# Attention followed by an MLP-mixer on one core: giving every engine a fixed order and preparing q and k pair by pair, several pairs ahead

## The chip, the cores and the metric

The kernel runs on one core of a Trainium2 chip. The metric is the device time of one execution in microseconds (us). Every number below comes from such a run, or from the trace of one profiled execution. The trace's own length, from the first to the last recorded instruction, is called the span; in every execution on record it is 1.7 to 2.5 us shorter than that execution's device time.

The engines are named as in the profile: PE does matrix multiplications (PEld is its loading of weights), DVE is the vector engine, ACT the one for activation functions, POOL is GpSimd, and SP issues most of the loads. Each engine works through its own list of instructions in order. An instruction that waits for another engine holds up everything behind it on its own list: in a timeline below, a sum that waits 6.64 us on DVE holds up a copy that was long ready. Two memories are named: PE writes its results into PSUM, and other engines copy them out; the other tiles lie in SBUF.

## The reference

```python
# B=8 batches, H=12 heads, S=448 positions, E=64; D = H*E = 768
q_n = q / (norm(q, axis=-1) + 1e-06)
k_n = k / (norm(k, axis=-1) + 1e-06)
attn = softmax(q_n @ k_n.T / tau)             # tau = 0.1
x = (attn @ v).transpose(0, 2, 1, 3).reshape(B, S, D)

h = relu(x.T @ w_tok1) @ w_tok2               # 448 -> 256 -> 448, over the positions
u = x + h.T
out = u + relu(u @ w_ch1) @ w_ch2             # 768 -> 1536 -> 768, over the channels
```

## The kernel before

The twelve heads of a batch are six pairs, so there are 48 pairs in all; three pairs make a half batch ("half"), of which there are 16. A round is one pass of the loop, for one pair. For each pair, PE transposes the normalised q and k (`tpose`), computes scores in two groups (`score`), ACT takes their exponential, and PE multiplies by v (`pv`). The mixer's work for a batch is queued when its attention is done and is fed to PE in small portions between the parts of later pairs. Before any of it, q and k must be normalised. This is called preparation here: squares, their sums, a square root by way of Ln and Exp, a reciprocal, and the scaling.

```python
def prep(n, lo, hi, sq_eng):                     # a whole half at a time
    ...
    for i, src in enumerate((qf, kf)):
        ...
            nc.gpsimd.tensor_mul(out=sq[:, i], in0=src, in1=src)
    nc.vector.tensor_reduce(out=ssq[:], in_=sq[:]..., axis=AXX.X, op=ALU.add)
    nc.scalar.activation(out=nr[:], in_=ssq[:], func=AF.Ln, bias=tiny[:])
    nc.scalar.activation(out=nr[:], in_=nr[:], func=AF.Exp, scale=0.5)
    nc.vector.tensor_scalar_add(out=rnf, in0=nr[:], scalar1=EPS_NORM)
    nc.vector.reciprocal(out=rnf, in_=rnf)
    for j in range(lo, hi, 2):                   # three pairs
        ...                                      # qn, kn <- q, k times rn, on GpSimd

def score(i, cg):                                # twice for each pair; psS has one buffer
    ...
    nc.scalar.activation(out=st["pt"][:, cg], in_=psS[:, :, :, 0:S], func=AF.Exp, scale=inv_tau)

with tc.manual_schedule(engines={PE, mybir.EngineType.Pool}):
    ...
    for i in range(NP_ALL + 1):
        ...
        if i % HP == 2 and i // HP + 2 < NHALF:
            prep(i // HP + 2, 0, 6, "pool")
            cast_v(i // HP + 2)                  # on DVE
        ...
            score(i, 0)
            left = feed(left + quota * 0.25)     # mixer work of an earlier batch
            if i:
                pv(i - 1, 0)
            ...
```

PE and GpSimd follow the order of the program text; the order on DVE and ACT is chosen by a scheduler when the kernel is built.

Of the kernel before, what the change touches and what calls it, by code (L numbers as in the profile page):

```python
# [7 lines left out]
FP32 = mybir.dt.float32  # L8
FP16 = mybir.dt.float16
AF = mybir.ActivationFunctionType  # L10
ALU = mybir.AluOpType
AXX = mybir.AxisListType
PE = mybir.EngineType.PE

ACT_SET_LN_EXP = 6

# [1 line left out]
def _bcast_free(ap: bass.AP, n: int) -> bass.AP:  # L18
    new_ap = list(ap.ap) + [[0, n]]
    return bass.AP(tensor=ap.tensor, offset=ap.offset, ap=new_ap)  # L20
# [3 lines left out]
def kernel(  # L24
# [12 lines left out]
    nc = tc.nc  # L37

    B, H, S, E = q.shape
# [3 lines left out]
    SC = 112  # L43
    NCH = S // SC
# [6 lines left out]
    HP = 3  # L51
# [5 lines left out]
    COLS = (0, 128, 256, S - 128)  # L57

    cst = ctx.enter_context(tc.tile_pool(name="cst", bufs=1))
    stage = ctx.enter_context(tc.tile_pool(name="stage", bufs=1))  # L60
    qkv = ctx.enter_context(tc.tile_pool(name="qkv", bufs=2))
    nrm = ctx.enter_context(tc.tile_pool(name="nrm", bufs=2))
    att = ctx.enter_context(tc.tile_pool(name="att", bufs=3))
    ptp = ctx.enter_context(tc.tile_pool(name="ptp", bufs=3))
    xp = ctx.enter_context(tc.tile_pool(name="xp", bufs=2))
    mix = ctx.enter_context(tc.tile_pool(name="mix", bufs=2))
    outp = ctx.enter_context(tc.tile_pool(name="outp", bufs=3))
# [19 lines left out]
    NV = 3  # L87
# [28 lines left out]
            nc.gpsimd.dma_start(out=wc2t[:, 6 * i:6 * i + 6, :],  # L116
                                in_=moe_w_ch2[768 * i:768 * (i + 1)].rearrange("(t p) d -> p t d", p=128))

    def load_half(n, split=False):
        b, h0 = n // 2, 6 * (n % 2)  # L120
        qt = qkv.tile([SC, 6, NCH, E], FP32, name=f"qh_{n}", tag="qh")
        kt = qkv.tile([SC, 6, NCH * E], FP32, name=f"kh_{n}", tag="kh")
        vs = qkv.tile([SC, 6, NCH * E], FP32, name=f"vs_{n}", tag="vs")
        for lo, hi in (((0, 2), (2, 6)) if split else ((0, 6),)):
            nc.sync.dma_start(out=qt[:, lo:hi].rearrange("p g c e -> p (g c) e"),
                              in_=q[b, h0 + lo:h0 + hi].rearrange("g (c p) e -> p (g c) e", p=SC))
            nc.sync.dma_start(out=kt[:, lo:hi],
                              in_=k[b, h0 + lo:h0 + hi].rearrange("g (p c) e -> p g (c e)", c=NCH))
        nc.sync.dma_start(out=vs[:], in_=v[b, h0:h0 + 6].rearrange("g (p c) e -> p g (c e)", c=NCH))
        half[n] = dict(q=qt, k=kt, vs=vs, vt=vts[n % NV])  # L130

    def prep(n, lo, hi, sq_eng):

        hf = half[n]
        g = hi - lo
        qf = hf["q"][:, lo:hi].rearrange("p g c e -> p (g c) e")
        kf = hf["k"][:, lo:hi].rearrange("p g (c e) -> p (g c) e", e=E)
        sq = nrm.tile([SC, 2, g * NCH, E], FP32, name=f"sq_{n}_{lo}", tag="sq", bufs=1)
        for i, src in enumerate((qf, kf)):
            if sq_eng == "act":  # L140
                nc.scalar.activation(out=sq[:, i], in_=src, func=AF.Square)
            else:
                nc.gpsimd.tensor_mul(out=sq[:, i], in0=src, in1=src)  # L143
        ssq = nrm.tile([SC, 2 * g * NCH], FP32, name=f"ssq_{n}_{lo}", tag="ssq")
        nc.vector.tensor_reduce(out=ssq[:], in_=sq[:].rearrange("p a g e -> p (a g) e"),  # L145
                                axis=AXX.X, op=ALU.add)
        nr = nrm.tile([SC, 2 * g * NCH], FP32, name=f"nr_{n}_{lo}", tag="nr")
        nc.scalar.activation(out=nr[:], in_=ssq[:], func=AF.Ln, bias=tiny[:])
        nc.scalar.activation(out=nr[:], in_=nr[:], func=AF.Exp, scale=0.5)
        rn = nrm.tile([SC, 2, g, NCH], FP32, name=f"rn_{n}_{lo}", tag="rn")  # L150
        rnf = rn[:].rearrange("p a g c -> p (a g c)")
        nc.vector.tensor_scalar_add(out=rnf, in0=nr[:], scalar1=EPS_NORM)
        nc.vector.reciprocal(out=rnf, in_=rnf)
        for j in range(lo, hi, 2):
            qn = att.tile([SC, NCH, 2, E], FP16, name=f"qn_{n}_{j}", tag="qn")
            kn = att.tile([SC, NCH, 2, E], FP16, name=f"kn_{n}_{j}", tag="kn")
            for i, (dst, src) in enumerate(((qn, hf["q"][:, j:j + 2]),
                                            (kn, hf["k"][:, j:j + 2].rearrange("p g (c e) -> p g c e", e=E)))):
                nc.gpsimd.tensor_tensor(out=dst[:].rearrange("p c g e -> p g c e"), in0=src,  # L159
                                        in1=_bcast_free(rn[:, i, j - lo:j - lo + 2], E), op=ALU.mult)  # L160
            pipe[3 * n + j // 2] = dict(qn=qn, kn=kn)

    def cast_v(n):
        hf = half[n]
        nc.vector.tensor_copy(out=hf["vt"][:, :, :, 0:E].rearrange("p g c e -> p (g c) e"),  # L165
                              in_=hf["vs"][:].rearrange("p g (c e) -> p (g c) e", e=E))

    def tpose(i):
        st = pipe[i]
# [134 lines left out]

    NP_ALL = B * NPAIR
    queue = []

    def feed(budget):

        while queue and budget > queue[0][0] / 2:  # L310
            t, fn = queue.pop(0)
            fn()
            budget -= t
        return budget

    with tc.manual_schedule(engines={PE, mybir.EngineType.Pool}):
        load_half(0, split=True)
        prep(0, 0, 2, "act")
        load_half(1)
        prep(0, 2, 6, "act")  # L320
        cast_v(0)
        weights_tok()
        prep(1, 0, 6, "pool")
        cast_v(1)
        weights_ch1()
        tpose(0)
        for i in range(NP_ALL + 1):
            b, pj = i // NPAIR, i % NPAIR
            left = 0.0
            if i % HP == 1 and i // HP + 2 < NHALF:  # L330
                load_half(i // HP + 2)
            if i % HP == 2 and i // HP + 2 < NHALF:
                prep(i // HP + 2, 0, 6, "pool")
                cast_v(i // HP + 2)
            if i == 2:
                weights_ch2()
            quota = sum(t for t, _ in queue) / (NPAIR - pj + 1) if queue else 0.0
            if i == NP_ALL:
                pv(i - 1, 0)
                pv(i - 1, 1)  # L340
            else:
                score(i, 0)
                left = feed(left + quota * 0.25)
                if i:
                    pv(i - 1, 0)
                left = feed(left + quota * 0.25)
                if i + 1 < NP_ALL:
                    tpose(i + 1)
                score(i, 1)
                left = feed(left + quota * 0.25)  # L350
                if i:
                    pv(i - 1, 1)
                left = feed(left + quota * 0.25)
            if pj == 0 and i:
                first, second = mixer_units(b - 1)
                queue += braid(first, out_units(b - 2) if b >= 2 else []) + second
        queue += out_units(B - 1)
        feed(1e9)
# [35 lines left out]
```

## Time and profile before

| | before |
|---|---|
| device time, median of 3 runs (lowest to highest) | 551.6 us (551.0 to 552.3) |
| span of the profiled execution | 547.6 us |
| PE busy | 445.7 us, 81% |
| first matmul of the mixer (psR) | 66.2 us after the start |
| from there to the end of the span | 481.5 us |
| time at half clock, as far as recorded | 85.6 us |

These are lines of the page of the kernel before: part 1 (busy time and share of the span for each engine), part 2 (40 equal slices; a digit is the busy share in tenths, and PEclk is the granted clock), and part 4 (the chain of work that ended last, by engine).

```profile
...
PE 445.7 (81%) x4136; PEld 267.8 (49%) x4136; DVE 225.7 (41%) x415; ACT 235.7 (43%) x259; POOL 186.7 (34%) x145
...
PE   1546884977997889697977969889795999999996
...
PEclk9999586989898979899896989989897999999999
...
PE 59%; POOL 16%; DVE 14%; issue 5%; ACT 4%; DMA 1%; POOLq 0%; ACTq 0%
...
```

PE is busy for 81%, and nothing else comes near. But only 59% of the chain is PE: another 30% is GpSimd and DVE, which means that the end of the kernel waited for their work and not for PE's. The clock row dips again and again.

The windows of the kernel before (length, then the busy us of each engine with its instruction count, then granted clock, DMA share and GB/s):

```profile
...
80.00:120.00 40.00, 27.43 (x283) 15.89 (x281) 18.54 (x33) 20.61 (x23) 22.96 (x16) 0.83 0.42 96
...
400.00:440.00 40.00, 32.58 (x313) 19.00 (x311) 14.71 (x29) 18.89 (x21) 13.59 (x10) 0.87 0.06 21
440.00:480.00 40.00, 40.00 (x411) 25.15 (x408) 15.42 (x36) 18.00 (x18) 2.05 (x2) 1.00 0.12 41
...
```

After 440 us, when no preparation is left, PE is busy all the time at full clock.

The timeline around the last preparation of the kernel before shows why (start, us, engine, line, operation, tiles written and read; in brackets, how long the engine had been idle and who released it):

```profile
...
411.41 2.75 POOL L143 TENSOR_TENSOR sq_0_4734<-qh_4596 112x1536 f32<-112x1536 f32 x1
...
414.11 2.75 POOL L143 TENSOR_TENSOR sq_0_4734<-kh_4597 112x1536 f32<-112x1536 f32 x1
416.89 3.35 DVE L145 TENSOR_REDUCE ssq_0_4737<-sq_0_4734 112x48 f32<-112x3072 f32 x1 [6.64 <-POOL sq_0_4734 L143]
...
420.25 0.59 DVE L243 CAST ut_2_3774<-psU_5_4718 128x448 f16<-128x448 f32 x1
...
420.90 0.53 PE L249 MATMUL psG_0_4726<-ut_2_3774,wc1t 128*128 128x448 f16 x1 [6.67 <-DVE ut_2_3774 L243]
...
```

GpSimd squares q and k of a whole half, 2.75 us each. DVE stands idle in front of the sum for 6.64 us, because the sum is next on its list, and then needs 3.35 us for it. Behind the sum stands the copy `ut_2`, which empties a PSUM tile of the mixer and which PE needs. PE therefore waits for 6.67 us. Afterwards it runs at half clock: the six matmuls of the psG group that follows at 422 us take 2.36 us of the chain, and 1.14 us where the clock is full. The Trainium skill, "TensorE: Matmul & The Clock Gate", Part 1, has it that an idle window of about 3.4 us drops the PE to half its clock, and that about 3.4 us of work restore it. The size agrees: in this trace the half clock comes in stretches of 3.4, 6.8, 10.2 and 13.7 us.

The longest waits of PE from 66 to 440 us in the kernel before (tile, line, releaser; total us, times, longest us):

```profile
...
PE psG_0_911 L249 <- DVE ut_0_766 L243: 8.2, 1, 8.2
PE psG_0_3243 L249 <- DVE ut_1_2291 L243: 6.7, 1, 6.7
PE psG_0_4726 L249 <- DVE ut_2_3774 L243: 6.7, 1, 6.7
...
```

All waits of PE in this stretch add up to 63 us, and most of the long ones are of this kind: 48 of the 63 us fall into times in which DVE waits for the squares of a whole half or is summing them.

### The profile page before, as it was taken

Reading aid. Unit: us, or ns where it says so; the run is one execution under the profiler, and the core shown is the slowest. Engines: PE = TensorE matmul, PEld = TensorE weight load, DVE = VectorE, ACT = ScalarE, POOL = GpSimd, SP = SyncE. Lnnn points to the kernel's source line nnn. Section 1 sums busy time; section 2 is a strip of 40 time slices with the busy share of each in tenths; the row PEclk is TensorE's granted clock in tenths of the full one; section 3 lists DMA queues with packets and bytes.
Section 4 is the critical chain, followed back from the end, with each engine's and each line's share of the span. In section 5 each row is a group of like instructions: output and inputs, shape, how many; then the busy total and the mean of one; then the engine's idle time right before and its main releaser. Section 6 shows DMA issues by size and latency. Waiting matters only on the chain.

```text
span 547.6 us, 9482 instructions
## 1 busy us (share of the span) xinstructions
PE 445.7 (81%) x4136; PEld 267.8 (49%) x4136; DVE 225.7 (41%) x415; ACT 235.7 (43%) x259; POOL 186.7 (34%) x145
## 2 busy tenths in 40 slices
PE   1546884977997889697977969889795999999996
PEld 0324552544653546354543536545462556656553
DVE  3468484355434344434434344433553233313100
ACT  4435442663346534274434733356343653451221
POOL 2854946525252513325251351515324210000000
PEclk9999586989898979899896989989897999999999
DMA  9969994614170604506070241802200001100102
GB/s 194 225 148 225 230 231 101 152 48 107 56 182 0 152 30 122 118 10 142 30 196 15 56 97 60 209 1 54 77 30 29 1 2 59 57 2 29 59 30 87
DMA packets 72841, 50.02 MB, mean 91 GB/s; under 512 B 44448, under 2 KB 68448, under 8 KB 72800
## 3 DMA queue, kind: packets, MB, share of 16 engines
q1 hardware_dynamic: 69408, 44.05, 32.9%
q0 software_dynamic: 3392, 5.37, 5.5%
q8 instruction: 32, 0.52, 0.4%
q14 instruction: 9, 0.07, 0.0%
HBM read 43.78 MB, written 11.01 MB: 100 GB/s over the span
## 4 chain that ended last, share of the span: by engine, by line
PE 59%; POOL 16%; DVE 14%; issue 5%; ACT 4%; DMA 1%; POOLq 0%; ACTq 0%
DVE vt_102 L165 2%; POOL sq_0_4330 L143 1%; POOL sq_0_3996 L143 1%; POOL sq_0_2847 L143 1%; POOL sq_0_3569 L143 1%; POOL sq_0_3251 L143 1%; POOL sq_0_2513 L143 1%; POOL sq_0_1086 L143 1%; POOL sq_0_776 L143 1%; POOL sq_0_2104 L143 1%; POOL sq_0_1382 L143 1%; POOL sq_0_4734 L143 1%; POOL sq_0_1776 L143 1%; PE psF_0_1_2161 L268 1%; DVE vt_100 L165 1%
## 5 line engine op out<-in xcount | busy, mean ns | idle before, releaser
L249 PEld LDWEIGHTS <-wc1t 128*128 128x128 f16 x576 | 53.9, 102 | 71.8 <-issue 31.0
L268 PEld LDWEIGHTS <-gt_0_767 128*128 128x128 f16 x168 | 16.1, 101 | 16.7 <-issue 7.7
L268 PEld LDWEIGHTS <-gt_1_2292 128*128 128x128 f16 x168 | 15.9, 101 | 14.3 <-issue 4.9
L268 PEld LDWEIGHTS <-gt_2_3775 128*128 128x128 f16 x168 | 15.6, 99 | 13.4 <-issue 3.9
L268 PEld LDWEIGHTS <-gt_3_5228 128*128 128x128 f16 x168 | 15.9, 98 | 9.6
L217 PEld LDWEIGHTS <-w1t 128*128 128x128 f16 x128 | 11.6, 102 | 13.7 <-issue 8.5
L249 PE MATMUL psG_0_911<-ut_0_766,wc1t 128*128 128x448 f16 x6 | 1.6, 384 | 8.2 <-DVE ut_0_766 L243 8.2
L173 PE MATMUL pst_188<-id_89,qn_0_127 112*128 112x112 f16 x4 | 0.6, 294 | 9.4 <-POOL qn_0_127 L159 9.4
L268 PE MATMUL psF_0_1_2161<-wc2t,gt_0_767 128*128 128x384 f16 x12 | 4.0, 520 | 4.6 <-DVE ost_0_2086 L274 4.6
L249 PE MATMUL psG_0_3243<-ut_1_2291,wc1t 128*128 128x448 f16 x6 | 1.6, 383 | 6.7 <-DVE ut_1_2291 L243 6.7
L249 PE MATMUL psG_0_4726<-ut_2_3774,wc1t 128*128 128x448 f16 x6 | 1.6, 382 | 6.7 <-DVE ut_2_3774 L243 6.7
L274 DVE COPY ost_0_5917<-psF_0_0_5918 128x384 f32<-128x384 f32 x1 | 0.6, 558 | 15.2 <-PE psF_0_0_5918 L271 15.2
L145 DVE TENSOR_REDUCE ssq_0_3572<-sq_0_3569 112x48 f32<-112x3072 f32 x1 | 3.4, 3352 | 7.1 <-POOL sq_0_3569 L143 7.1
L145 DVE TENSOR_REDUCE ssq_0_3254<-sq_0_3251 112x48 f32<-112x3072 f32 x1 | 3.4, 3353 | 6.6 <-POOL sq_0_3251 L143 6.6
L145 DVE TENSOR_REDUCE ssq_0_4737<-sq_0_4734 112x48 f32<-112x3072 f32 x1 | 3.4, 3352 | 6.6 <-POOL sq_0_4734 L143 6.6
L203 PEld LDWEIGHTS <-pt_800 112*128 112x128 f16 x32 | 1.7, 115 | 8.8 <-issue 8.7
L173 PE MATMUL pst_347<-id_89,qn_0_173 112*128 112x112 f16 x4 | 0.6, 294 | 6.6 <-POOL qn_0_173 L159 6.6
L145 DVE TENSOR_REDUCE ssq_0_779<-sq_0_776 112x48 f32<-112x3072 f32 x1 | 3.4, 3354 | 5.9 <-POOL sq_0_776 L143 5.9
L249 PE MATMUL psG_0_4035<-ut_2_3774,wc1t 128*128 128x448 f16 x6 | 1.8, 382 | 4.6 <-DVE ut_2_3774 L243 4.6
L249 PE MATMUL psG_0_2552<-ut_1_2291,wc1t 128*128 128x448 f16 x6 | 1.8, 382 | 4.6 <-DVE ut_1_2291 L243 4.6
L145 DVE TENSOR_REDUCE ssq_0_1779<-sq_0_1776 112x48 f32<-112x3072 f32 x1 | 3.4, 3352 | 5.0 <-POOL sq_0_1776 L143 5.0
L145 DVE TENSOR_REDUCE ssq_0_1385<-sq_0_1382 112x48 f32<-112x3072 f32 x1 | 3.4, 3352 | 5.0 <-POOL sq_0_1382 L143 5.0
(1637 smaller groups left out, 1311.0 us busy)
## 6 DMA issues: line engine op xcount, KB each, us to landing
wc1t<-in_moe_w_ch_dram POOLq DMA_DIRECT2D x2, 1152.0 KB, 14.3
wc2t<-in_moe_w_ch_dram POOLq DMA_DIRECT2D x2, 1152.0 KB, 17.6
vs_110<-in_v_dram SPq DMA_DIRECT2D x1, 672.0 KB, 7.9
qh_131<-in_q_dram SPq DMA_DIRECT2D x1, 672.0 KB, 10.9
kh_132<-in_k_dram SPq DMA_DIRECT2D x1, 672.0 KB, 13.0
vs_133<-in_v_dram SPq DMA_DIRECT2D x1, 672.0 KB, 8.7
qh_223<-in_q_dram SPq DMA_DIRECT2D x1, 672.0 KB, 6.5
kh_224<-in_k_dram SPq DMA_DIRECT2D x1, 672.0 KB, 10.3
```

Of the source, the lines that this page charges most:

```text
L143: nc.gpsimd.tensor_mul(out=sq[:, i], in0=src, in1=src)
L145: nc.vector.tensor_reduce(out=ssq[:], in_=sq[:].rearrange("p a g e -> p (a g) e"), axis=AXX.X, op=ALU.add)
L165: nc.vector.tensor_copy(out=hf["vt"][:, :, :, 0:E].rearrange("p g c e -> p (g c) e"), in_=hf["vs"][:].rearrange("p g (c e) -> p (g c) e", ...
L173: nc.tensor.transpose(pst[:, a, c, :], src[:, c], id16[:SC, :SC])
L203: nc.tensor.matmul(psO[:, m, 0:E + 1], st["pt"][:, c // 2, hh, c % 2, lo:lo + 128], vt[:, g, c, 0:E + 1], start=(c == 0), stop=(c == NCH - 1))
L217: nc.tensor.matmul(psR[:], w1t[:, m, tt * 128:(tt + 1) * 128], x16[b][:, m, dh * DH:(dh + 1) * DH], start=(m == 0), stop=(m == 3))
L249: nc.tensor.matmul(psG[:], wc1t[:, dt, ct * 128:(ct + 1) * 128], ut[:, dt, span(b)], start=(dt == 0), stop=(dt == DT - 1))
L268: nc.tensor.matmul(psF[:], rows(gt, ct), wc2t[:, ct, dh * DH:(dh + 1) * DH], start=(ct == 0), stop=False)
L274: nc.vector.tensor_copy(out=o[:, 0:DH], in_=psF[:])
```

## The change

The intent: no instruction on DVE or ACT should reach the head of its list before its input is there. For this the preparation is cut into stages of one pair. Squares are made six pairs ahead, at the beginning of a round; the sum of a pair stands at the end of the next round, so nearly two rounds behind its squares; reciprocals are made once per half, and scalings two pairs ahead. All engines follow the order of the text, so that the place of each piece is given. The cast of v to 16 bits goes from DVE to GpSimd. In the start, pairs are prepared one by one, with the squares of pair 0's q on ACT and the scaling of k for pairs 0 to 5 on DVE; in the kernel before, ACT made all squares of the first half. There is one buffer more for q and k, whose loads are issued earlier, and one less for the exponentials.

```diff
-    qkv = ctx.enter_context(tc.tile_pool(name="qkv", bufs=2))
+    qkv = ctx.enter_context(tc.tile_pool(name="qkv", bufs=3))
...
-    ptp = ctx.enter_context(tc.tile_pool(name="ptp", bufs=3))
+    ptp = ctx.enter_context(tc.tile_pool(name="ptp", bufs=2))
...                                                  # prep() goes; in its place:
+    def cast_v(n):
+        nc.gpsimd.tensor_copy(...)
+    def squares(i, act_q=False):                     # one pair: 2 x 512 columns
+        ...
+                nc.gpsimd.tensor_mul(out=sq[:, a], in0=src, in1=src)
+    def sums(i):                                     # one pair, on DVE
+        ...
+    def rnorms(n, p0=0, p1=HP):                      # Ln, Exp on ACT; + eps, reciprocal on DVE
+        ...
+    def scaled(i, dve_k=False):                      # one pair, on GpSimd
+        ...
...
-    with tc.manual_schedule(engines={PE, mybir.EngineType.Pool}):
+    with tc.manual_schedule():
...                                                  # the start, pair by pair
+        squares(0, act_q=True)
+        sums(0)
+        rnorms(0, 0, 1)
+        squares(1)
+        scaled(0, dve_k=True)
+        tpose(0)
+        squares(2)
+        sums(1)
+        rnorms(0, 1, 2)
+        cast_v(0)
+        score(0, 0)
+        scaled(1, dve_k=True)
+        tpose(1)
+        score(0, 1)
+        sums(2)
+        rnorms(0, 2, 3)
+        scaled(2, dve_k=True)
         weights_tok()
+        squares(3)
+        sums(3)
+        rnorms(1, 0, 1)
         for i in range(NP_ALL + 1):
...
-            if i % HP == 2 and i // HP + 2 < NHALF:
-                prep(i // HP + 2, 0, 6, "pool")
-                cast_v(i // HP + 2)
+            if i == 0:
+                squares(4)
+                scaled(3, dve_k=True)
+            if i == 1:
+                squares(5)
+                scaled(4, dve_k=True)
+                cast_v(1)
+                weights_ch1()
             if i == 2:
+                scaled(5, dve_k=True)
+            if i >= 4 and i + 2 < NP_ALL:
+                scaled(i + 2)
+            if 6 <= i + 6 < NP_ALL:
+                squares(i + 6)
+            if i == 6:
                 weights_ch2()
+            if (i + 3) % HP == 0 and 2 <= (i + 3) // HP < NHALF:
+                cast_v((i + 3) // HP)
...                                                  # score, feed, pv, tpose as before
+            if i < 2:
+                sums(4 + i)
+                rnorms(1, 1 + i, 2 + i)
+            if i >= 1 and i + 5 < NP_ALL:
+                sums(i + 5)
+                if (i + 5) % HP == 2:
+                    rnorms((i + 5) // HP)
```

The way in which mixer work is portioned out changed a little too: the shares of a round are 0.3, 0.2, 0.3 and 0.2 instead of four times 0.25, with at least 500 ns of work ahead of the transposes.

## The prediction

> **What bounds it now.** TensorE (PE) is the bottleneck, but starved: the page gives it 81% of a 547.6 us span. By the windows view, from 440 to 520 us PE is busy 100% at full granted clock; from 80 to 440 us it is busy 272.6 of 360 us, with the clock down to 0.83-0.87 in places. The chain of waits repeats one pattern per half batch: GpSimd squares 5.4 us, DVE reduction 3.35, then PE. The timeline around 411-421 us shows why: DVE waits 6.6 us for the squares, with a PSUM copy (ut) behind it that PE needs; PE waits 6.7 us, then runs at half clock (448-column matmuls every 375 instead of 189 ns). This agrees with the Trainium skill, "TensorE: Matmul & The Clock Gate", Part 1: an idle window of about 3.4 us halves the clock. The clock is at half for some 85 us in 15 stretches.
>
> Before 66 us only attention work exists: score, exponential 1.66 us, score, 5.5 us a pair, plus three interruptions of 4-7 us by preparation (v casts of 3.7-4.8 us on DVE beside GpSimd squares; 0.93 alone).
>
> **The change.** Matmuls and bytes stay. Squares come in 512-column pieces, six pairs ahead; sums 1.2 us a pair; reciprocals are ready before a half's first pair. No DVE or ACT instruction should then hold up PSUM evictions. GpSimd per pair: 2x0.95 squares + 2x1.04 scalings + a third of a cast [...] = 4.7 us, against about 8 us for a steady pair. DVE and ACT stay near 5, so PE should bind. DVE still waits once per half for Ln/Exp (0.31+0.22 us) behind ACT's queue: an estimated 1-2 us, mostly covered by four PSUM buffers.
>
> **Sum.** Median full-clock issue intervals of all PE groups add up to 383 us. Stretches free of preparation (140-160, 200-220, 440-480) work at 97% of that.
> - Start: first score at about 13 us (11.7 now), as GpSimd takes pair 1's squares before pair 0's scaling. GpSimd then binds: cast, weight issues of 3 us and squares delay pair 1's exponentials to about 27, pair 2's to 34; then 5.5 us a pair. First mixer matmul at 61 us (now 66).
> - Then 367 us of PE work at 96-97%: 380 us.
> - Tail 3, cold clock 2; time exceeds span by 4.
>
> 61 + 380 + 3 + 2 + 4 = 450 us, ratio 0.82. Some 95 of the 101 us lie in 66-440 us: stalls and the half clock behind them.
>
> Range 436 to 475 us. Chances: faster 0.97, same 0.02, slower 0.01.
>
> **What would show the steps right or wrong.**
> - Chain of waits: squares and reductions vanish after 70 us; PE rises from 59% to over 85%.
> - Windows: PE at least 95% busy, clock 1.0, from 70 us on.
> - Waits: no PE wait on ut or qn over 3 us after 70 us.
> - Page: GpSimd busy 215-225 us, DVE about 200; PE share over 90%, its busy time falling to about 410.
> - First mixer matmul at 58-65 us.
>
> **What would make it wrong.** In the start, loads (DMA at its limit until 80 us) or GpSimd's fixed order push the first mixer matmul past 70 us. In the steady state, ACT's or DVE's fixed order blocks evictions at each group of reciprocals, 2-3 us a half, giving 92% and about 470 us. Or the GpSimd cast takes far over 2 us. Idle windows that remain keep the half clock.

One figure in it is wrong: the windows of the kernel before give 298.6 of 360 us from 80 to 440 us, not 272.6. The sum does not use it. In the 4.7 us for GpSimd, the cast's share was a guess that no trace stood behind; the cast then took 1.46 us.

## The result, and the profile after

| | before | after |
|---|---|---|
| device time, median of 4 runs (lowest to highest) | 551.86 us (551.04 to 552.28) | 469.74 us (469.30 to 470.67) |
| span of the profiled execution | 547.6 us | 468.7 us |
| first mixer matmul | 66.2 us | 69.0 us |
| from there to the end of the span | 481.5 us | 399.7 us |
| time at half clock, as far as recorded | 85.6 us | 6.4 us |

The changed kernel takes 0.8516 of the time (95% interval 0.8499 to 0.8532). A ratio is the mean time of one kernel's runs over that of the other's of the same rounds, so it is not quite the ratio of the medians. The time lies within the predicted range, but 20 us above the predicted 450 us. The last four rows come from the profiled executions, and all the gain lies behind the first mixer matmul. The start became 2.8 us longer.

The page of the kernel after, the same lines:

```profile
...
PE 418.2 (89%) x4136; PEld 257.6 (55%) x4136; DVE 219.1 (47%) x442; ACT 232.4 (50%) x262; POOL 219.0 (47%) x220
...
PE   0405879999999999999999999999999999999995
...
PEclk9999999999999999999999999999999999999999
...
PE 84%; ACT 6%; DVE 4%; POOL 2%; issue 2%; DMA 1%; SPq 0%; ACTq 0%; POOLq 0%
...
```

The chain is now PE for 84%, and the clock row has no dip left. Of the 6.4 us, 3.0 us come after the last matmul and cost nothing. The windows of the kernel after:

```profile
...
0.00:60.00 60.00, 24.80 (x238) 16.39 (x239) 31.53 (x52) 22.63 (x27) 42.93 (x51) 1.00 1.06 211
...
80.00:120.00 40.00, 38.59 (x437) 24.10 (x435) 23.00 (x50) 28.06 (x30) 28.73 (x28) 1.00 0.59 126
...
200.00:240.00 40.00, 38.86 (x418) 24.39 (x418) 21.47 (x45) 22.49 (x24) 22.10 (x22) 1.00 0.38 89
...
```

From 80 us on PE is busy for at least 38.6 of every 40 us until its last window, at full clock. The 1.00 in the first window is not to be believed, however. The clock records of each trace begin with the first rise to full clock, here at 61.8 us and in the kernel before at 48.0 us. Two groups of 16 matmuls of `pv` in the kernel after, from the start and from later:

```profile
...
21.67 1.06 PE L213 MATMUL psO_0_259<-vt_97,pt_165 112*128 112x65 f16 x16
...
150.57 0.69 PE L213 MATMUL psO_1_2008<-vt_101,pt_1842 112*128 112x65 f16 x16
...
```

Before the first record, the matmuls of such groups begin 54 to 55 ns apart (the median of each group) in all fourteen traces, as where half clock is recorded; at full clock they begin 32 to 33 ns apart. So the start ran at half clock without a record of it, and "half clock" in the tables leaves this out. It matters for the pace: where nothing else held them up, exponentials in the kernel after follow each other by 2.73 to 2.75 us before 61.8 us, and by 2.34 to 2.40 us just after it. The 5.5 us a pair in the prediction is the pace at half clock.

The waits of PE for another engine after 75 us in the kernel after (tile, line, releaser; total us, times, longest us) begin like this:

```profile
...
PE psS_0_2815 L198 <- ACT pt_2723 L200: 1.1, 1, 1.1
PE psS_0_1336 L198 <- ACT pt_1236 L200: 1.1, 1, 1.1
...
```

There are six of this kind and one of 0.2 us; a seventh of 1.1 us ends at 68.3 us, just before the first mixer matmul. No wait for a PSUM copy or for a normalised q is left, only short ones for an exponential. One stands at the change from each batch to the next. There the previous batch's queue is used up, the next batch's has not been filled yet, and two score groups of the single psS buffer follow each other with nothing but a `pv` between them.

What went less well is in the first 60 us. This is a part of the timeline of the kernel after:

```profile
...
19.03 1.66 ACT L200 ACTIVATE pt_165<-psS_1_187 112x1792 f16<-112x1792 f32 x1 [2.52 <-PE psS_1_187 L198]
20.59 0.30 ACT L164 ACTIVATE rn_109<-ssq_108,tiny 112x16 f32<-112x16 f32 x1
...
21.71 1.55 POOL L175 TENSOR_TENSOR qn_198<-qh_105,rn_109 112x512 f16<-112x512 f32 x1 [4.63 <-DVE rn_109 L167]
...
23.45 0.93 POOL L100 DMA_DIRECT2D w1t<-in_moe_w_tok_dram  x1
...
26.38 1.05 POOL L152 TENSOR_TENSOR sq_207<-qh_115 112x512 f32<-112x512 f32 x1
...
28.47 1.22 DVE L157 TENSOR_REDUCE ssq_118<-sq_207 112x16 f32<-112x1024 f32 x1 [6.11 <-POOL sq_207 L152]
...
29.72 0.31 ACT L164 ACTIVATE rn_119<-ssq_118,tiny 112x16 f32<-112x16 f32 x1 [8.59 <-DVE ssq_118 L157]
...
32.66 0.31 ACT L164 ACTIVATE rn_119<-ssq_118,tiny 112x16 f32<-112x16 f32 x1 [2.39 <-DVE ssq_118 L157]
...
33.12 1.65 ACT L200 ACTIVATE pt_251<-psS_0_252 112x1792 f16<-112x1792 f32 x1
...
34.82 0.99 PE L198 MATMUL psS_1_290<-qk_185 64*112 64x448 f16 x4 [10.58 <-ACT pt_251 L200]
...
```

Read it from the bottom. PE waits for 10.58 us with the second score of pair 1, because the psS buffer still holds the first one, whose exponential runs only at 33.12 us. That exponential could have run at about 21.7 us. But in ACT's fixed order the Ln and Exp of pairs 3 and 4 (29.72 and 32.66 us) stand in front of it; these wait for sums, and the sums for squares that GpSimd starts only at 26.38 us. GpSimd is late because it idled for 4.63 us in front of pair 2's scaling, whose Ln stood on ACT behind pair 0's second exponential, and then issued weight loads for about 3 us.

A second hold-up, also from the timeline of the kernel after:

```profile
...
40.70 4.68 DVE L175 TENSOR_TENSOR kn_324<-kh_116,rn_119 112x512 f16<-112x512 f32 x1
40.79 1.05 POOL L152 TENSOR_TENSOR sq_248<-qh_123 112x512 f32<-112x512 f32 x1
...
43.79 1.03 POOL L152 TENSOR_TENSOR sq_326<-qh_123 112x512 f32<-112x512 f32 x1
...
44.79 1.49 POOL L152 TENSOR_TENSOR sq_326<-kh_124 112x512 f32<-112x512 f32 x1
...
46.52 0.99 PE L198 MATMUL psS_0_400<-qk_365 64*112 64x448 f16 x4 [3.72 <-DVE qk_365 L185]
...
```

The scaling `kn_324` on DVE takes 4.68 us; four of the five others take 0.69 us. GpSimd runs five instructions without a pause beside it. DVE ends 0.6 us after the fifth has begun, and the fifth takes 1.49 instead of 1.05 us; so DVE seems to have been let in between the fourth and the fifth. The Trainium skill, "SBUF — State Buffer", section "SBUF: two separate sides", calls the pair of memory ports that DVE and GpSimd share an exclusive lock: the one that starts first has it for its whole instruction, and the other is fully blocked. It counts DVE operations with two SBUF inputs among those that need it. This trace agrees in that one of the two was held up and not slowed a little, and it adds a size: the blocked DVE instruction was let in not after one GpSimd instruction but, by these times, after four. Which of the two came first it does not show: the DVE record begins 0.09 us before that of the first square. PE waited 3.72 us for the copy behind it.

### The profile page after: what moved, and what is told of

It is laid out like the page before. It is cut to its first block, busy times and chain, and to the rows that moved or that the text cites. A ratio compares the mean times of both kernels' runs of the same rounds, so it can differ in the third digit from the quotient of the medians.

```text
span 468.7 us, 9522 instructions
## 1 busy us (share of the span) xinstructions
PE 418.2 (89%) x4136; PEld 257.6 (55%) x4136; DVE 219.1 (47%) x442; ACT 232.4 (50%) x262; POOL 219.0 (47%) x220
## 4 chain that ended last, share of the span: by engine, by line
PE 84%; ACT 6%; DVE 4%; POOL 2%; issue 2%; DMA 1%; SPq 0%; ACTq 0%; POOLq 0%
DMA qh_105<-in_q_dram 1%; DVE kn_324 L175 1%; DVE ssq_118 L157 1%; ACT pt_630 L200 1%; ACT pt_482 L200 1%; ACT pt_1042 L200 1%; DVE ssq_126 L157 0%; POOL sq_207 L152 0%; PE psF_2_1_5429 L278 0%; PE psF_2_0_5377 L278 0%; PE psF_2_1_4787 L278 0%; PE psF_1_0_4581 L278 0%; PE psF_0_1_4513 L278 0%; PE psF_2_1_3968 L278 0%; PE psF_2_0_3897 L278 0%
## 5 line engine op out<-in xcount | busy, mean ns | idle before, releaser
L259 PEld LDWEIGHTS <-wc1t 128*128 128x128 f16 x576 | 51.5, 98 | 51.1 <-issue 9.8
L278 PEld LDWEIGHTS <-gt_2_3862 128*128 128x128 f16 x168 | 15.3, 98 | 12.5 <-issue 2.4
L278 PEld LDWEIGHTS <-gt_1_2351 128*128 128x128 f16 x168 | 15.4, 98 | 12.2 <-issue 2.4
L278 PEld LDWEIGHTS <-gt_0_804 128*128 128x128 f16 x168 | 15.5, 98 | 11.2 <-issue 1.4
L278 PEld LDWEIGHTS <-gt_3_5342 128*128 128x128 f16 x168 | 15.9, 98 | 9.6
L198 PE MATMUL psS_1_290<-qk_185 64*112 64x448 f16 x4 | 1.0, 574 | 10.6 <-ACT pt_251 L200 10.6
L164 ACT ACTIVATE rn_119<-ssq_118,tiny 112x16 f32<-112x16 f32 x3 | 0.9, 307 | 12.1 <-DVE ssq_118 L157 12.1
L183 PEld LDWEIGHTS <-qn_141 112*128 112x128 f16 x4 | 0.3, 129 | 11.6 <-POOL qn_141 L175 11.6
L175 POOL TENSOR_TENSOR qn_5044<-qh_4311,rn_4315 112x512 f16<-112x512 f32 x1 | 1.0, 1042 | 10.4 <-DVE rn_4315 L167 10.4
L164 ACT ACTIVATE rn_109<-ssq_108,tiny 112x16 f32<-112x16 f32 x3 | 0.9, 304 | 9.2 <-DVE ssq_108 L157 9.2
L175 DVE TENSOR_TENSOR kn_324<-kh_116,rn_119 112x512 f16<-112x512 f32 x1 | 4.7, 4685 | 0.0
L281 PEld LDWEIGHTS <-ut_3_5341 128*128 128x128 f16 x42 | 3.5, 98 | 1.8
L281 PEld LDWEIGHTS <-ut_0_803 128*128 128x128 f16 x42 | 3.5, 98 | 1.8
L281 PEld LDWEIGHTS <-ut_1_2350 128*128 128x128 f16 x42 | 3.5, 98 | 1.8
L281 PEld LDWEIGHTS <-ut_2_3861 128*128 128x128 f16 x42 | 3.5, 98 | 1.8
L175 POOL TENSOR_TENSOR qn_3954<-qh_3191,rn_3195 112x512 f16<-112x512 f32 x1 | 1.0, 1043 | 7.3 <-DVE rn_3195 L167 7.3
L198 PE MATMUL psS_0_400<-qk_365 64*112 64x448 f16 x4 | 1.0, 598 | 3.7 <-DVE qk_365 L185 3.7
L152 POOL TENSOR_TENSOR sq_2301<-qh_2033 112x512 f32<-112x512 f32 x1 | 1.0, 1041 | 6.9 <-DVE ssq_1701 L157 6.9
```

Of the source, the lines that this page charges most:

```text
L152: nc.gpsimd.tensor_mul(out=sq[:, a], in0=src, in1=src)
L164: nc.scalar.activation(out=rn, in_=ssq, func=AF.Ln, bias=tiny[:])
L175: eng.tensor_tensor(out=dst[:].rearrange("p c g e -> p g c e"), in0=src, in1=_bcast_free(rn, E), op=ALU.mult)
L183: nc.tensor.transpose(pst[:, a, c, :], src[:, c], id16[:SC, :SC])
L198: nc.tensor.matmul(psS[:, hh, j, 0:S], qk[hb:hb + 64, 1, c * SC:(c + 1) * SC], qk[hb:hb + 64, 0, :], start=True, stop=True)
L259: nc.tensor.matmul(psG[:], wc1t[:, dt, ct * 128:(ct + 1) * 128], ut[:, dt, span(b)], start=(dt == 0), stop=(dt == DT - 1))
```

## The experiments

Two theories stood at the beginning for the 82 us behind the first mixer matmul. The first: preparation is cut into pieces and moved ahead, so that no long wait stands in front of a copy out of PSUM. The rival: what matters is that DVE and ACT have a given order. Later runs split the first: is it the distance between squares and sums, or the small pieces? For the missing 20 us two more were to be told apart: preparation still in the way of PE, or PE's own work and the start costing more than was reckoned. Each run was timed together with the kernel before on the same chip, so ratios are to that kernel; its median was 551.3 to 552.0 us in all of these sets. "Rest" is the stretch from the first mixer matmul to the end of the span in the profiled execution, which can lie off the median: by 3.2 us in auto_order and by 2.2 us in k5_pool, both times above. "Half clock" is what is recorded; it lacks the start, and in each run its last 2 to 5 us lie behind the last matmul.

| run | median us | ratio, 95% interval | first mixer matmul | rest | half clock |
|---|---|---|---|---|---|
| before | 551.86 | 1 | 66.2 | 481.5 | 85.6 |
| after | 469.74 | 0.8516, 0.8499 to 0.8532 | 69.0 | 399.7 | 6.4 |
| auto_order | 484.61 | 0.8788, 0.8734 to 0.8842 | 70.5 | 415.5 | 47.3 |
| before_hand | 580.40 | 1.0499, 1.0431 to 1.0567 | 90.2 | 490.0 | 101.0 |
| before_bufs | 545.46 | 0.9885, 0.9833 to 0.9937 | 65.1 | 478.0 | 82.6 |
| whole_half | 486.15 | 0.8825, 0.8798 to 0.8852 | 71.6 | 414.2 | 5.8 |
| near | 478.45 | 0.8679, 0.8646 to 0.8712 | 69.9 | 406.7 | 16.5 |
| cast_dve | 469.88 | 0.8512, 0.8463 to 0.8561 | 68.4 | 398.3 | 16.3 |
| no_norms | 465.60 | 0.8453, 0.8425 to 0.8481 | 64.8 | 398.0 | 6.1 |
| k5_pool | 467.64 | 0.8481, 0.8455 to 0.8507 | 67.9 | 400.0 | 2.7 |
| start2 | 462.34 | 0.8392, 0.8373 to 0.8412 | 57.8 | 402.7 | 4.9 |
| start3 | 460.60 | 0.8350, 0.8311 to 0.8389 | 52.8 | 407.7 | 31.8 |
| fill | 464.41 | 0.8441, 0.8407 to 0.8476 | 67.2 | 395.1 | 3.4 |
| best | 452.77 | 0.8216, 0.8187 to 0.8245 | 52.0 | 398.4 | 13.3 |

All gave right results except no_norms.

### auto_order: the kernel after, with DVE and ACT ordered by the scheduler again

```diff
@@ -330 +330 @@
-    with tc.manual_schedule():
+    with tc.manual_schedule(engines={mybir.EngineType.PE, mybir.EngineType.Pool}):
```

> The changed kernel with the hand-given order kept on PE and GpSimd only; DVE and ACT are ordered by the scheduler again, as in the kernel before. Theory A (the gain comes from the preparation being cut into stages and moved ahead, so that no long wait stands in front of a PSUM eviction): 462 to 480 us, no PE wait over 3 us after 75 us. Rival B (the gain is the hand-given order of DVE and ACT): 510 us or more.

The time is 484.61 us, between what the two theories asked for, 4.6 us above the range of the first. The rest grows from 399.7 to 415.5 us, so of the 82 us gained there about 66 remain without the given order. What the order gives is seen in the timeline of auto_order:

```profile
...
318.92 1.22 DVE L157 TENSOR_REDUCE ssq<-sq 112x16 f32<-112x1024 f32 x1 [3.30 <-POOL sq L152]
...
```

The scheduler puts the sum on DVE's list at the time when its squares begin, so DVE idles in front of it again, though for 3.30 instead of 6.64 us, because the squares of one pair take about 2 and not 5.5 us. Of the 47.3 us at half clock 40.9 us lie before 76 us, in and just after the start, where the kernel after ran mostly at half clock too, without a record.

### before_hand: the kernel before, with all engines in the order of the text

```diff
@@ -316 +316 @@
-    with tc.manual_schedule(engines={PE, mybir.EngineType.Pool}):
+    with tc.manual_schedule():
```

> The kernel before with hand-given order on all engines, preparation unchanged. Theory A: the reduction over a half batch still stands in front of the pair's evictions and waits for GpSimd, so 530 to 565 us with PE waits of 5 us or more once per half. Rival B: below 500 us.

This is slower than before, by 5%, and 15 us above the range that I expected: the start takes 24 us more and the rest 8.5 us more. From the timeline of before_hand:

```profile
...
349.91 3.35 DVE L145 TENSOR_REDUCE ssq<-sq 112x48 f32<-112x3072 f32 x1 [3.09 <-POOL sq L143]
...
353.30 0.34 ACT L148 ACTIVATE nr<-ssq,tiny 112x48 f32<-112x48 f32 x1 [7.66 <-DVE ssq L145]
...
355.51 0.99 PE L188 MATMUL psS<-qk 64*112 64x448 f16 x4 [4.99 <-ACT pt L190]
...
```

The sum of the whole half comes at its place in the text, while its squares are still running; the Ln waits for the sum for 7.66 us with the exponential of the attention behind it, and PE waits for that exponential for 4.99 us. PE's waits for an exponential add up to 63.4 us in this run. A given order is no gain in itself. It makes a badly placed instruction block with certainty.

### before_bufs: the kernel before, with six instead of three buffers for the normalised q and k

```diff
@@ -155,2 +155,2 @@
-            qn = att.tile([SC, NCH, 2, E], FP16, name=f"qn_{n}_{j}", tag="qn")
-            kn = att.tile([SC, NCH, 2, E], FP16, name=f"kn_{n}_{j}", tag="kn")
+            qn = att.tile([SC, NCH, 2, E], FP16, name=f"qn_{n}_{j}", tag="qn", bufs=6)
+            kn = att.tile([SC, NCH, 2, E], FP16, name=f"kn_{n}_{j}", tag="kn", bufs=6)
```

> The kernel before with six buffers instead of three for the scaled q and k, nothing else. If GpSimd's squares come late because its scalings wait for PE to free these buffers (waits of 5 to 12 us on the transposes), this alone removes most of the stalls: 480 to 510 us. If the cause is only the place of the reduction in DVE's order: 535 us or more.

Here my theory was that in the kernel before GpSimd could not run ahead for want of buffers: it waits up to 12.1 us for a transposition by PE before it may write the next `qn`. The theory fell: 545.46 us, only 1.2% faster. GpSimd still waited for PE's transpositions for 153.8 us in 23 waits, and PE still waited for `ut` behind a sum for up to 7.9 us. DVE still stood waiting for squares in front of 12 sums, for 62.3 us in all (68.1 us in 13 in the kernel before).

### whole_half: the kernel after, with squares and sums of a whole half in single instructions

In the text, the sums stand nearly three rounds behind the squares (two in the kernel after); the given order stays.

```diff
+    def squares_half(n):
+        ...                                         # two instructions of 1536 columns
+    def sums_half(n):
+        ...                                         # one reduction of 3072 columns
...
-            if 6 <= i + 6 < NP_ALL:
-                squares(i + 6)
+            if i % HP == 1 and 2 <= (i + 5) // HP < NHALF:
+                squares_half((i + 5) // HP)
...
             if i >= 1 and i + 5 < NP_ALL:
-                sums(i + 5)
                 if (i + 5) % HP == 2:
+                    sums_half((i + 5) // HP)
                     rnorms((i + 5) // HP)
```

> The changed kernel with squares and sums of a whole half batch in single instructions again (two squares of 1536 columns, one sum of 3072) from half 2 on, but still in hand-given order and with the sums two pairs after the squares. If the distance between a producer on GpSimd and its consumer in the fixed order of DVE is what counts: 465 to 480 us, no PE wait over 3 us after 80 us, although DVE's sum takes 3.35 us. If cutting the work into pairs is what counts: 490 us or more, with DVE waits of 3 us or more for the squares.

The rest is 414.2 us, 14.5 more than with small pieces, and 67 less than before. So the time lies just beyond the one expectation and below the other. From the timeline of whole_half:

```profile
...
243.43 3.34 DVE L168 TENSOR_REDUCE ssq<-sq 112x48 f32<-112x3072 f32 x1
...
246.81 0.33 ACT L181 ACTIVATE rn<-ssq,tiny 112x48 f32<-112x48 f32 x1 [4.53 <-DVE ssq L168]
...
248.59 0.36 PE L200 MATMUL pst<-id,qn 112*128 112x112 f16 x4 [1.33 <-DVE ost L301]
...
```

DVE does not wait for the squares any more: the sum has no bracket. But it takes 3.34 us in one piece, the Ln waits for it, the exponential stands behind the Ln, and PE loses 1.33 us. The half clock does not come back (5.8 us in all). So without the small pieces, but with the distance and the given order, the long stalls are gone, and with them the half clock; the small pieces are worth another 14.5 us, seen as short stalls.

### near: the kernel after, with sums and reciprocals directly behind the squares

```diff
@@ -381,2 +381,8 @@
                 cast_v((i + 3) // HP)
+            if i >= 7:
+                for j in ((12, 13) if i == 7 else (i + 6,)):
+                    if j < NP_ALL:
+                        sums(j)
+                        if j % HP == 2:
+                            rnorms(j // HP)
             quota = sum(t for t, _ in queue) / (NPAIR - pj + 1) if queue else 0.0
@@ -403,3 +409,3 @@
                 rnorms(1, 1 + i, 2 + i)
-            if i >= 1 and i + 5 < NP_ALL:
+            if 1 <= i < 7:
                 sums(i + 5)
```

> The changed kernel with the distance taken away: from pair 7 on the sums (and, where a half is complete, logarithm, exponential and reciprocal) of a pair stand directly after its squares at the head of the same round, in front of that round's exponentials and evictions, instead of one round later. The start is as it was. If the distance is needed: first mixer matmul to end 410 us or more (now 399.7), with waits of DVE for the squares. If GpSimd runs far enough ahead of PE by itself, so that cutting alone does it: 398 to 403 us, 468 to 474 us in all.

The rest is 406.7 us, 7 more than after, in the gap between the two expectations. The timeline of near shows where it is lost:

```profile
...
75.57 1.22 DVE L157 TENSOR_REDUCE ssq<-sq 112x16 f32<-112x1024 f32 x1 [3.14 <-POOL sq L152]
...
76.70 1.01 DVE L229 TENSOR_SCALAR rt<-psR 128x384 f16<-128x384 f32 x2
77.30 0.53 PE L183 MATMUL pst<-id,qn 112*128 112x112 f16 x4 [3.23 <-DVE rt L229]
...
```

At 75 us, when GpSimd is still catching up from the start, DVE waits 3.14 us for squares and PE 3.23 us behind it. Two stretches of half clock of 6.8 us lie around it, at 66 and 77 us, where the kernel after has one of 3.4 us. An estimate: 3.2 us of waiting and half of the 10.2 us more at half clock make 8 us, about the 7 measured. From 84 us on, near does as well as after: in the windows PE is busy for 314.3 of the 320 us from 120 to 440 us, in both. So the distance in the text is not needed as long as GpSimd in fact runs ahead, and it does so by itself from 84 us on. It is insurance for the time when GpSimd is behind.

### cast_dve: the kernel after, with the cast of v back on DVE

```diff
@@ -137 +137 @@
-        nc.gpsimd.tensor_copy(out=half[n]["vt"][:, :, :, 0:E].rearrange("p g c e -> p (g c) e"),
+        nc.vector.tensor_copy(out=half[n]["vt"][:, :, :, 0:E].rearrange("p g c e -> p (g c) e"),
```

> The changed kernel with the v cast back on DVE. Theory A: worth 0 to 5 us, so 468 to 475 us; single casts take 1 to 5 us where GpSimd is at work and 0.93 elsewhere. Rival C (the cast's move is a main part of the gain): 485 us or more.

Nothing changes: 469.88 us. The cast takes 0.9 to 1.8 us on DVE here, so the 5 us that I thought possible did not occur, and 1.46 to 1.48 us on GpSimd. The Trainium skill, "GPSIMD Engine Reference", section 4.1 "Engine selection", has GpSimd about twice as slow as the vector engine for elementwise operations with two inputs, and "roughly line-rate" for those with one. This agrees only in part: the scaling, with two inputs, takes 1.04 us against 0.69 us, and the cast, with one, 1.46 us against a median of 0.95 us. This part of the change was of no account for the time.

### no_norms: the kernel after, without squares, sums, Ln, Exp and reciprocals from the third half on

The factors are set to 1, so the output is wrong. GpSimd still scales.

```diff
@@ -377 +377 @@
-                squares(i + 6)
+                pipe[i + 6] = {}
@@ -405 +404,0 @@
-                sums(i + 5)
@@ -407 +406 @@
-                    rnorms((i + 5) // HP)
+                    nc.vector.memset(half[(i + 5) // HP]["rn"][:], 1.0)
```

> Wrong result on purpose: the changed kernel without squares, sums, logarithm, exponential and reciprocal from half 2 on; the reciprocal norms are set to 1, all else stays. If PE work alone binds after the start, nothing is left to gain there: the stretch from the first mixer matmul to the end stays at 400 us (now 69.0 to 468.7) within 5 us, and only the start can get shorter by a few us. If what remains of the preparation still costs PE time (my 380 us of PE work were right): the stretch shrinks to 380 to 388 us.

The rest is 398.0 us, against 399.7 us with the preparation. So squares, sums and reciprocals cost the steady part of the kernel after no more than about 2 us (the scalings and casts stayed in and are not tested by this), and what is left there is mostly PE's own work with its waits for the exponential.

### k5_pool: the kernel after, with pair 5's scaling of k on GpSimd

```diff
@@ -373 +373 @@
-                scaled(5, dve_k=True)
+                scaled(5)
```

> The changed kernel with one instruction moved: the scaling of k of pair 5 goes from DVE to GpSimd. If that instruction's 4.68 us on DVE (0.69 us for its likes) is waiting for GpSimd's back-to-back work and lies on the chain of the start: first mixer matmul 3 to 4 us earlier (65 to 66 us), 465 to 467 us in all. If it only fills a gap: 469 to 470 us.

The long DVE instruction is gone, and pair 3's exponential comes at 45.5 instead of 47.6 us. The median is 2.1 us lower in five rounds, but the intervals of the ratios overlap, and the first mixer matmul comes at 67.9 us, not at the 65 to 66 that I expected. In this execution the clock became full only at 71.5 us, against 61.8 us in the kernel after, which may hide a part. That the hold-up goes when k leaves DVE is shown, its worth is not.

### start2: the start rebuilt

ACT squares pairs 1 to 5, GpSimd scales first, weight loads and the squares of pairs 6 to 8 come later, and reciprocals are made pair by pair until pair 11.

```diff
-        squares(0, act_q=True)
+        side(0, 0, "act")                # one side of one pair, on the engine named
+        side(0, 1)
         sums(0)
         rnorms(0, 0, 1)
-        squares(1)
         scaled(0, dve_k=True)
+        for j in (1, 2):
+            for s in (0, 1):
+                side(j, s, "act")
         tpose(0)
-        squares(2)
         sums(1)
         rnorms(0, 1, 2)
-        cast_v(0)
         score(0, 0)
...
+                score(i, 0)
+                if i < 4:
+                    side(i + 2, 1, "act")
...
+                score(i, 1)
+                if i < 4:
+                    sums(i + 2)
+                    rnorms(1, i - 1, i)
+                    if i < 3:
+                        side(i + 3, 0, "act")
+                    scaled(i + 2)
...
```

> The changed kernel with another start: ACT, idle there, squares q and k of pairs 1 to 5, GpSimd scales pair 0 before anything of pair 1, the weight issues and the squares of pairs 6 to 8 come later, each pair has its own reciprocals until pair 11. The steady state is as it was. If the late first mixer matmul (69.0 instead of the predicted 61 us) comes from GpSimd's fixed order and the ACT order behind it: first mixer matmul at 47 to 54 us, 448 to 458 us in all. If loads set the pace of the start: first mixer matmul at 60 us or later, 462 us or more.

The first mixer matmul comes at 57.8 us, 11 us earlier than after, but later than the 47 to 54 that I expected. Pair 1's exponential starts at 20.2 instead of 33.1 us. The rest is 3 us longer, so the time falls by 7.4 us. About 2 us of the 3 are the clock, by an estimate: it became full only at 61.8 us, so the rest began with 4 us at half clock. That the arrangement of the start cost these microseconds is shown. How much of that is order and how much the squares' move to ACT is not, and the 462 us lie where I had expected them if loads set the pace; that is not ruled out.

### start3: start2, with transposes behind the second score and with reciprocals behind the next exponential

```diff
-        tpose(1)
         score(0, 1)
+        tpose(1)
...
+                for n, p in late:                # reciprocals of one pair, one round later
+                    rnorms(n, p, p + 1)
...
-                if i and i + 1 < NP_ALL:
+                if i >= 7 and i + 1 < NP_ALL:
                     tpose(i + 1)
                 score(i, 1)
+                if i < 7:
+                    tpose(i + 1)
...
```

> As start2, but in the start the transposes of the next pair stand after the second score instead of before it, and reciprocals of single pairs stand behind the next pair's first exponential instead of in front of it. In start2 PE waited for GpSimd's scaling in front of the second score and ACT for the sums in front of the exponentials. If order sets the pace: 5.5 to 5.7 us a pair, first mixer matmul at 47 to 51 us, 452 to 457 us in all. If loads or GpSimd set it: first mixer matmul at 55 us or later, 460 us or more.

The first mixer matmul comes at 52.8 us, again 5 us earlier, but the rest grows by another 5 us to 407.7 us. The time is only 1.7 us below that of start2, within the spread of the runs. The clock differs too: it was full from 48.4 us on, 13 us earlier than in start2. From the timeline of start3, it can be seen where the gain was given back:

```profile
...
62.25 3.70 DVE L175 TENSOR_SCALAR rn<-rn 112x16 f32<-112x16 f32 x1 [0.91 <-ACT rn L174]
62.90 1.04 POOL L152 TENSOR_TENSOR sq<-qh 112x512 f32<-112x512 f32 x1
...
64.89 1.03 POOL L152 TENSOR_TENSOR sq<-qh 112x512 f32<-112x512 f32 x1
...
66.16 1.08 DVE L262 CAST ut<-psU 128x448 f16<-128x448 f32 x2
66.77 0.44 PE L192 MATMUL pst<-id,qn 112*128 112x112 f16 x3 [4.36 <-DVE ut L262]
...
```

A tiny DVE instruction, the addition of epsilon on 16 columns, takes 3.70 us instead of 0.17: once more it sits behind GpSimd work without a pause. The copy `ut` stands behind it, PE waits 4.36 us, and a stretch of 6.8 us at half clock follows.

### fill: the kernel after, with the next batch's mixer work queued half a round earlier

Some of it runs before the next score.

```diff
@@ -399,3 +399,6 @@
                     pv(i - 1, 1)
-                feed(quota * 0.2)
+                if pj == 0 and i:
+                    first, second = mixer_units(b - 1)
+                    queue += braid(first, out_units(b - 2) if b >= 2 else []) + second
+                feed(quota * 0.2, 1300.0 if pj == 0 and i else 0.0)
             if i < 2:
@@ -407,3 +410,3 @@
                     rnorms((i + 5) // HP)
-            if pj == 0 and i:
+            if i == NP_ALL:
                 first, second = mixer_units(b - 1)
```

> The changed kernel, with the next batch's mixer units put into the queue half a step earlier and one of them run between the last product with v of a round and the next score, at each batch's first round. If the seven waits of PE for an exponential of 1.1 us each (8.0 us in all) are only a matter of where the matmul units stand: 461 to 464 us. If the waits move elsewhere: 468 to 471 us.

The time is 464.41 us in six runs, and the rest falls by 4.6 us to 395.1 us. These are all waits of PE after 75 us in fill:

```profile
...
PE psS L198 <- ACT pt L200: 1.2, 3, 0.6
```

They add up to 1.2 us, where the kernel after had six of 1.1 us. A first one, ending at 73.3 us, became longer (1.8 us). That the batch changes cost PE about 5 us is thereby shown.

### best: start3 and fill together

> start3 and fill together. The two lie in different stretches, so the gains should add: 445 to 450 us.

The time is 452.77 us (451.95 to 453.74 in four runs), 3 us more than I expected at most. It beats both kernels: its ratio to the kernel before is 0.8216, against 0.8516, which makes it about 3.5% faster than the kernel after (0.8216 / 0.8516, by way of the kernel before, since they ran on different chips). The windows of best:

```profile
...
0.00:60.00 60.00, 36.81 (x387) 24.60 (x388) 34.75 (x75) 38.24 (x49) 41.36 (x51) 0.91 1.10 220
...
80.00:440.00 360.00, 358.16 (x3515) 217.87 (x3513) 164.79 (x342) 186.69 (x214) 154.78 (x149) 1.00 0.36 88
...
```

From 80 to 440 us PE is busy for 358.2 of 360 us. What is left is the start: PE is busy for 36.8 of the first 60 us (24.8 in the kernel after). The chain of best has a load of q that takes 22.9 us from 55 us on, while the DMA share is at its limit (over 1). So the next gain may lie in the order of the loads. That was not tried.

## Why the prediction was right or wrong

Point by point:

- **Chain of waits.** Predicted: squares and reductions vanish after 70 us, and PE rises over 85%. Measured: PE 84%, POOL from 16 to 2%, DVE from 14 to 4%. Right but for the last percent.
- **Windows.** Predicted: PE at least 95% busy at full clock from 70 us on. Measured: 38.6 to 40.0 of 40 us from 80 us on, at clock 1.00. From 70 to 80 us PE is busy all the time, but the clock is full only from 72.0 us on. Right but for these 2 us.
- **Waits.** Predicted: none on `ut` or `qn` over 3 us after 70 us. Measured: none on these after 70 us, and none of any kind over 1.2 us. Right.
- **Page.** GpSimd is busy for 219 us (predicted 215 to 225), right. DVE is busy for 219 instead of about 200 us: missed. PE is busy for 418 instead of about 410 us, 89% instead of over 90%: narrowly missed.
- **First mixer matmul.** Predicted 61 us, in 58 to 65; measured 69.0. Missed.

The sum shows which terms were mis-sized. The measured column is the profiled execution, 470.67 us:

| term | predicted us | measured us |
|---|---|---|
| start, to the first mixer matmul | 61 | 69.0 |
| PE work to the last matmul's end, cold clock included | 380 + 2 | 394.7 |
| tail, to the end of the span | 3 | 5.1 |
| outside of the span | 4 | 2.0 |
| sum | 450 | 470.7 |

That the measured 470 us is also the "about 470 us" which the prediction gives for blocked evictions is chance: no such wait was found. The 4 us outside of the span came from setting the median of three runs (551.6 us) against the span of another, faster one (547.6 of its 549.74 us).

The first step that failed is "GpSimd then binds: cast, weight issues of 3 us and squares delay pair 1's exponentials to about 27, pair 2's to 34". The direction was right: the exponentials came at 33.1 and 39.1 us. But the count took only GpSimd's work, and not the circle through ACT's fixed order: GpSimd idled for 4.63 us behind an exponential, and then the exponential of pair 1 stood behind the Ln of pairs 3 and 4. Also, the 4.68 us of `kn_324` was not in it, though the profile before had shown the like (a cast of 4.81 us beside GpSimd squares). With start2, which changes all of this at once, the first mixer matmul came at 57.8 us.

The second step that failed is "Then 367 us of PE work at 96-97%: 380 us". It measured 394.7 us. What is mis-sized is the base, the 367 us. A group of matmuls (those of one tile and one line, such as the four of a score) can be timed from its first start to the start of the next group. With the median of each kind of group at full clock, the work from the first mixer matmul on adds up to 381 us, and the medians of the kernel before are the same as those of the kernel after to within 1 ns, so the 381 us could have been had beforehand. Against 394.7 us that is 97%, the efficiency that was predicted. Why the base came out low is not on record; medians of single matmuls, whose intervals differ within a group, give anything from 364 to 382 us here, by how they are sorted. Of the 14 us between 381 and 394.7, 7.0 us are waits for an exponential, six of them at batch changes, which the prediction did not have; fill won most of that back (4.6 us of the rest). Some 2 us are half clock, and the other 5 us are small excesses in many groups, not explained. That squares, sums and reciprocals are not the cause is shown by no_norms (398.0 against 399.7 us).

As to where the 82 us behind the first mixer matmul came from: the stalls of DVE in front of whole-half sums, and the half clock behind them, were the cause, as predicted: 48 of the 63 us of waits lay in them, the runs that keep them (before_hand, before_bufs) win nothing or little, and every run without them keeps at least 66 us. But no single part of the change carries the gain. Undoing the order of DVE and ACT (auto_order) gives 16 of the 82 us back; there the sums stand close behind their squares again, but the pieces are small. Undoing the small pieces (whole_half) gives 14.5 us back; there the sums are long, but stand nearly three rounds behind. Each keeps 66 to 67 us, so the two cures overlap. The waits show how: after 75 us, PE's longest wait is 2.0 us in auto_order and 2.3 us in whole_half (18 and 20 us in all), where it was 8.2 us before, and each has just one stretch of 3.4 us at half clock before its end, where the kernel before has 68 us in 13 stretches. Either cure alone keeps the stalls too short for the clock to drop. An estimate of the whole: the kernel before lost 63 us to waits, 56 more than after, and half of those 68 us, that is 34 us, to the half clock. That makes 90 us, a little over the 82 measured, as PE also waits in part of the time at half clock. The order alone, in the old arrangement, loses time (before_hand), and more buffers alone win little (before_bufs). What remains open is how much of the 66 us that both kernels keep is due to what they share with the changed kernel: the scalings of one pair at a time in GpSimd's order, the third buffer of q and k with its earlier loads, and the changed portions of mixer work. No run took these apart.

## What to carry to other kernels

When an engine of little load stalls the busiest one, look for the instruction at which it waits and for what stands behind it in its order: let the producer run ahead, and cut the piece so that its own length hides; here a kernel with either of the two, beside what all these runs share, kept most of the gain. A fixed order on all engines pays only after that; it turns each badly placed instruction into a certain stall, above all in the start, where nothing runs ahead yet. Keep independent work of the busiest engine in hand for the rounds where its queue runs dry, and check a won start for what is given back later.

## What the Trainium skill lacked or had wrong

- "SBUF — State Buffer", section "SBUF: two separate sides", says that the one that loses the shared ports is fully blocked for the other's instruction. It does not say that the loser can be passed over several times. In these runs a DVE scaling took 4.68 instead of 0.69 us beside five GpSimd instructions of about 1 us each, without a pause between them; a cast took 4.81 instead of 0.93 us; and an addition on 16 columns took 3.70 instead of 0.17 us.
- "TensorE: Matmul & The Clock Gate", section "Back-to-back issue gap", gives about 131 ns for each matmul in a sustained stream of 512 columns and says that its formula N/2.4 + 2.5 ns counts too much at large N. Here a stream of six 448-column matmuls takes 1.14 us of the chain, 190 ns each, and one of twelve with 384 columns 1.95 us, 163 ns each. The formula gives 189 and 162.5 ns, so it fits, and the smaller figure does not.
- "GPSIMD Engine Reference", section 4.1, calls operations with one input "roughly line-rate" on GpSimd and those with two about twice as slow as on the vector engine. The cast of 1536 columns took 1.46 us on GpSimd and 0.95 us on DVE, and a scaling of 512 columns 1.04 us and 0.69 us, each 1.5 times.
- "TensorE: Matmul & The Clock Gate", Part 1, does not say how little work makes a window idle. In the fourteen traces the clock changes at multiples of 3.41 us, counted from the first record. Before each of 52 drops, PE had been busy for at most 58% of the 3.41 us before, as the profile counts it, and in 38 of them for a tenth or more; of windows at full clock with over 58%, none was followed by a drop, and between 52 and 58% there were both. Before each of 52 rises it was at least 85%.
